# A fused attention and max-out kernel: one pair of loads ahead of the output weights, one product moved within a step, a table copied by GpSimd

## The chip, the cores and the metric

The kernel runs on one core of one Trainium2 chip. The time is the device time of one execution in microseconds (us). A core has five engines that run side by side, each with its instructions in a fixed order: TensorE (PE, with its weight loads shown apart as PEld), VectorE (DVE), ScalarE (ACT), GpSimd (POOL) and SyncE (SP). Data moves by DMA, issued here by SP (which also issues the DMA transposes) and by GpSimd (loads that turn float32 into bfloat16 on the way); ACT issues a few at the start.

## The reference

Two layers, the second fed by the first. There are 8 batches, 8 heads, 576 positions and 64 numbers a head:

```
scores = q @ k.T / 8 + bias[head, |i - j|]        # bias from a table of 32 buckets
x      = softmax(scores) @ v                      # (8 * 576) rows x 512
h      = max(x @ w1, x @ w2, x @ w3)              # 512 -> 768
out    = h @ w_out                                # 768 -> 512, float32
```

The bias depends only on the distance of two positions, and beyond a distance of 128 it is one constant. So exp(score + bias) is exp(score) times a factor that differs from one only in a band around the diagonal.

## The kernel before

**Tiles and steps.** Heads go in pairs. A step is one batch `b` and one pair `hp` (0 to 3). A batch's 576 positions are four tiles of 128 and 64 left over. In a step PE multiplies keys by queries in PSUM (`sc` for the main tiles, `sct` for the left-over keys, `scq` for the left-over queries), ACT writes the exponentials to SBUF (`e` for the main tiles, `el` for what is left over), VectorE multiplies the band by its factors (`times_band` and `times_band_pair`, lines 797 to 818, `times_bandt`, line 900, `times_band_left`, line 912), and PE multiplies by the values with a column of ones (`a`); VectorE then divides by that column's sum (`rd`, `x_sb`, lines 956 and 957). The product and the division of a step run during the next one (`attend`, line 920, called through `next_late`). `sc`, `sct` and `scq` take turns in two PSUM banks of the pool `ps_s`; ACT must have read a bank before PE writes it anew.

**Between these** stand the matmuls of the second layer for an earlier batch, in portions that `fill(target, *hooks)` (line 703) takes from a list: so many matmuls, with each hook (a product of the current step) called ahead of the last portion, or between two, and behind them if none is left. For the first batches the gates' tiles are `ps`, later `psp`; the products with the output weights are `pso`. The first of the latter come in the step of batch 2, pair 1, and read `wo_bf`.

**Band factors.** `hank` holds, for each head, the factors along the diagonals; it is read backwards. `bandt` holds the part for the left-over keys, copied once by `make_bandt` (line 346): two copies of 64 partitions by 768 numbers, each read backwards. In the kernel before, VectorE makes it in the first pass over batch 0's second halves (line 1152), before the first quotients. Its first reader is `times_bandt` of batch 0's first pair, line 901 in the profile.

**Loads.** From batch 2 on a batch's q and k come pair by pair: `load_pair(b, g)` issues two q and two k loads of 64 KB from GpSimd (line 189), `load_left` the left-over rows. `begin_qk(b)` issues pair 0, the left-over rows and pair 1, `end_qk(b)` pairs 2 and 3. Every load of a batch from 2 on goes through `in_turn` (line 150): once a list is open (`paced`, from batch 1 on), it waits for the sixth load before it to land. The weights' loads go through the same call with b = 0 and neither wait nor count. In the step of batch 1, pair 1, GpSimd issues the values of batch 2 (four main loads and two tails), then the output weights (`load_last_weights`, line 1079, 768 KB), then pairs 2 and 3 of batch 2. Two steps' code later come the loads for batch 3.

**Transposes.** From batch 2 on SP transposes q and k by DMA (line 725; left-over rows at line 732) at places written out by hand (`places`, line 1193): batch 2's pair 0 and left-over rows in the step of batch 1, pair 1, its pair 1 in that of pair 2, its third pair in that of batch 1, pair 3, its fourth pair in that of batch 2, pair 1. Between those two places stand the five transposes of batch 1's result, x to xT (line 967), two for the first half and three for the second. SP takes all of them in this order, and the stores of the output too. In this text "third pair" and "fourth pair" are the pairs of batch 2 with the numbers 2 and 3.

**The step of batch 2, pair 0** is the last one of its kind (no gates from a stage list, `rate` 8). There the left-over keys' product is not called in the first `fill`, as in other steps, but in the last one of the step, together with `times_bandt` (`late_keys`, `late_products`).

At the start, `load_second` (line 1066) issues batch 1's q and k in packed form (line 241), with left-over rows and the second weight matrix in between, has GpSimd spread the first pair (`spread_packed`, two copies, line 246), and issues batch 1's values and the third weight matrix.

Of the kernel before, what the change touches and what calls it, by code (L numbers as in the profile page):

```python
# [39 lines left out]
def kernel(  # L40
# [12 lines left out]
    nc = tc.nc  # L53
# [6 lines left out]
    HP = H // 2  # L60
# [63 lines left out]
    def dve_copy(out_, in_):  # L124
        return inorder(nc.vector.tensor_copy(out_, in_))
# [58 lines left out]
    def load_pair(b, g):  # L184

        for src, dst in zip((q, k), batch[b]):
            for par in range(2):
                part = main_part(src, b)[:, :, 2 * g + par, :]
                in_turn(b, nc.gpsimd.dma_start(out=dst[:, g, :, par, :], in_=part))  # L189
# [10 lines left out]
        load_left(b)  # L200
        load_pair(b, 1)

    def end_qk(b):
        for g in range(2, HP):
            load_pair(b, g)

    def go_behind(loads, behind):

        for load in loads if behind else ():
# [6 lines left out]
    def load_v(b, h0, h1):  # L216
        load_main(v, b, h0, h1, vx[b % 2][:, :, :, 0:D])
        load_tail(v, b, h0, h1, v_diag)
# [24 lines left out]
    def spread_packed(hp, eng):  # L243
        h = slice(2 * hp, 2 * hp + 2)
        for dst, src in zip(batch[1], (q_1, k_1)):
            inorder(eng.tensor_copy(dst[:, :, h, :], src[:, h].rearrange("p h t d -> p t h d")))
# [99 lines left out]
    def make_bandt():  # L346
        for par in range(2):
            r = slice(64 * par, 64 * par + 64)
            c = BAND // 2 - 64 * par
            dve_copy(bandt[r, :, :], hank[r, par::2, c : c + 192][:, :, ::-1])  # L350

# [546 lines left out]
    def times_bandt(hp, el):  # L900
        return inorder(nc.vector.tensor_tensor(
            out=el[:, S - 192 : S], in0=el[:, S - 192 : S], in1=bandt[:, hp, :], op=ALU.mult
        ))
# [153 lines left out]
    def load_w(i):  # L1057
        src = (moe_w1, moe_w2, moe_w3)[i].rearrange("(c p) f -> p c f", p=P)
        for f0, f1 in ((0, QS), (QS, d_ff)) if i else ((0, d_ff),):
            in_turn(0, nc.gpsimd.dma_start(out=w_bf[i][:, :, f0:f1], in_=src[:, :, f0:f1]))  # L1060
# [5 lines left out]
    def load_second():  # L1066
        for h0, h1 in ((0, 2), (2, H)):
            load_packed(k, h0, h1, k_1)
            load_packed(q, h0, h1, q_1)
            if h0 == 0:  # L1070
                load_q_tail(1)
                load_tail(k, 1, 0, H, k_diag)
                load_w(1)
        spread_packed(0, nc.gpsimd)
        load_v(1, 0, H)
        load_w(2)
# [16 lines left out]
    for hp in range(HP):  # L1093
        qT, kT = (x[:, hp, :] for x in qk[0])
        e4, el = e_tiles()
# [29 lines left out]
    for hp in range(HP):  # L1125
        qT, kT = (x[:, hp, :] for x in qk[0])
        if begun:
            e4, el = begun.pop()
            more_transposes(hp + 1)
            scores(qT, kT, e4, 1, 2)  # L1130
        else:
            e4, el = e_tiles()
            visit(qT, kT, e4, [(1, 0), (1, 2)], (lambda: more_transposes(hp + 1)) if hp + 1 < HP else None)

        def keys():
            left_keys(hp, qT, kT, el, QS, S)

        def queries():
            left_queries(hp, qT, kT, el)

        def late_bands(hp=hp, e4=e4):
            times_band(hp, e4, 1, QS, QM, inorder)
            times_band_pair(hp, e4, 2, QS)

        if hp == 0:
            keys()
        if hp == 1:
            x_transposes(0, 0)
        quotients = next_late()
        if hp < 2:  # L1150
            if hp == 0:
                make_bandt()
            quotients()
            if hp == 0:
                bands(2)
            else:
                behind.pop()()
                keys()
            queries()
            if hp == 1:  # L1160
                x_transposes(1, 0)
            else:
                begun.append(e_tiles())
                scores(*(x[:, 1, :] for x in qk[0]), begun[0][0], 1, 0)
            quotients = next_late()
            quotients()
            if hp == 0:
                bands(3)
            behind.append(lambda late_bands=late_bands, hp=hp, el=el: (late_bands(), products(hp, el)))
        else:  # L1170
            if behind:
                behind.pop()()
            if hp == 3:
                quotients()
                add_ffn(0, QS)
                fill(8)
            keys()
            if hp == 2:
                quotients()
            queries()  # L1180
            late_bands()
            if hp == 2:
                x_transposes(2, 0)
                x_transposes(3, 0)
            else:
                begin_qk(2)
                x_transposes(0, 1)
                fill(8, lambda: second_transposes(qk[1], 0))
            products(hp, el)
        late.append(lambda hp=hp, e4=e4, el=el: attend(0, hp, e4, el, 1))  # L1190
# [15 lines left out]
    for b, hp in [(b, hp) for b in range(1, B) for hp in range(HP)]:  # L1206
# [54 lines left out]
        if rows:  # L1261
            begin2, end2 = thirds.pop()()
            if not run.keys_late:
                end_keys = left_keys_rows(qT, kT, el)
            begin2()
            if not run.keys_late:
                end_keys()
            if not lead:
                key_scores(qT, kT, e4, 2)
            largest = end2(2 if run.keys_late else 1)  # L1270

            def bands():
                times_band(hp, e4, 2, 0, QM, inorder)
                times_bandt(hp, el)
                times_band(hp, e4, 3, 0, QM, inorder)

            def left():
                left_queries(hp, qT, kT, el)
                times_band_left(hp, el)

            def ahead():
                n = HP * b + hp + 1
                if n < HP * B:
                    begun.append(e_tiles())
                    key_scores(*(x[:, n % HP, :] for x in qk[n // HP]), begun[0][0], 0)

            run(
                lambda: key_scores(qT, kT, e4, 3), left, ahead, largest, bands, lambda: left_keys_rows(qT, kT, el)
            )
            thirds.append(after)  # L1290
        elif tiled:
            if len(pending) > 1:
                fill(DCH)
            keys()
            fill(FCH)
            times_band(hp, e4, 0, 0, QS, inorder)
            begin0, end0, begin1, end1, alone = run
            scores(qT, kT, e4, *order[2])
            begin0()
            exp_left = left_queries(hp, qT, kT, el)  # L1300
            turned_1 = begin1()
            if (b, hp) == (3, 0):
                left_keys(hp, qT, kT, el, 0, S)
            times_band(hp, e4, 1, 0, QM, inorder)
            band_left = times_bandt(hp, el)
            go_behind([band_left], turned_1[-1])
            times_band_left(hp, el)
            scores(qT, kT, e4, *order[3])
            dve0 = end0([exp_left])
            dve1 = end1([band_left])  # L1310
            times_band(hp, e4, 2, 0, QM, inorder)
            dve0()
            times_band(hp, e4, 3, 0, QM, inorder)
            dve1()
            pending.extend((n, [fn]) for n, fn in alone)
        else:
            late_keys = (b, hp) == (2, 0)
            fill(8 if (b, hp) == (2, 1) else rate, (lambda: None) if late_keys else keys, *([lambda: None] if together else []))
            if b == 1 and hp + 1 < HP:
                spread_packed(hp + 1, nc.vector)  # L1320
            if not late_keys:
                times_bandt(hp, el)


            def beside_scores():
                banks = [pool.tile([P, KT * 64], F32, tag=tag, name="scq") for pool, tag in ((ps_a, "a"), (ps_f, "ff"))]
                turn_left_queries(qT, kT, banks)
                put_left_queries(el, banks)

            visit(qT, kT, e4, order[2:], None if together else beside_scores, el=el if together else None)  # L1330
# [15 lines left out]
        if hp == 1 and b + 1 < B:  # L1346
            paced.append(b)
            load_v(b + 1, 0, H)
            if b == 1:
                load_last_weights()  # L1350
            end_qk(b + 1)
        if hp == (2 if b == 1 else 1) and b + 2 < B:
            begin_qk(b + 2)

# [5 lines left out]
                times_band(hp, e4, t, 0, QM, inorder)  # L1360

        if not tiled:
            def late_products():
                keys()
                times_bandt(hp, el)

            fill(rate, *([late_products] if late_keys else []), bands_2, queries)
            times_band_left(hp, el)
        if hp == 1 and b > 1:
            stages.extend(made)  # L1370
# [56 lines left out]
```

## Time and profile before

| What | Value |
|---|---|
| median of three runs (lowest, highest) | 309.41 us (309.14, 309.49) |
| the profiled execution: its own time | 309.08 us |
| the profiled execution: its span | 307.3 us |
| PE busy | 296.4 us (96%) |
| VectorE busy | 208.4 us (68%) |
| ACT busy | 201.9 us (66%) |
| GpSimd busy | 141.2 us (46%) |
| loads from GpSimd's queue | 16.66 MB |
| granted TensorE clock, mean | 0.997 |

The profile is of one execution. A busy share is an average over the span; where an engine stands still, and for what, is in other views. The *waits* name, for an engine and a line, what ended its idle time (total, number of times, longest). The *timeline* lists instructions in order of time: start, length, engine, line, what is written and read; a note in brackets is the idle time ahead of it and what ended that. For a DMA the length is that of its issue on the engine; its data lands later, and the trace has the time from issue to landing as well. The *chain* follows the work that ended last back from the end. Engines with a q behind the name (SPq) are their instruction queues. Line numbers are those of the kernel before.

### The profile page before, as it was taken

The numbers are of one execution on the slowest core, as the hardware profiler recorded it, in microseconds if no ns is written. First come the engines' busy times: TensorE is split into PE (matmuls) and PEld (weight loads), VectorE is DVE, ScalarE is ACT, GpSimd is POOL, SyncE is SP. The second block draws the span as 40 slices with busy tenths as digits, with TensorE's granted clock in tenths as the row PEclk, the third lists the DMA queues.
The fourth block names the chain that finished last, engine by engine and source line by source line (L and its number), as shares of the span: only waits on it lengthen the run. The fifth ranks groups of instructions, "written<-read, shape, count | busy, mean of one in ns | idle before, by whom it ended". The sixth has DMA issues, their size and how long they took to land.

```text
span 307.3 us, 10608 instructions
## 1 busy us (share of the span) xinstructions
PE 296.4 (96%) x4547; PEld 182.0 (59%) x4547; DVE 208.4 (68%) x471; ACT 201.9 (66%) x273; POOL 141.2 (46%) x197
## 2 busy tenths in 40 slices
PE   7889999999899999999999999999999999999995
PEld 2367877765455655567666766676667654444442
DVE  7498888776677767676777677767777765453552
ACT  3999989887677677768776777777777730222211
POOL 8977778479677657856566826510000000000000
PEclk9999999999999999999999999999999999999998
DMA  9999999999999999999999999996323013202003
GB/s 162 200 187 191 167 140 130 177 113 161 218 179 168 141 189 210 99 142 208 171 113 146 208 166 90 140 196 105 71 45 119 26 36 82 97 2 102 34 0 137
DMA packets 165774, 40.48 MB, mean 132 GB/s; under 512 B 154584, under 2 KB 161248, under 8 KB 165728
## 3 DMA queue, kind: packets, MB, share of 16 engines
q0 software_dynamic: 105664, 16.66, 91.0%
q1 hardware_dynamic: 58304, 22.69, 37.3%
q8 instruction: 35, 0.57, 0.8%
q10 hardware_dynamic: 1760, 0.47, 0.7%
q14 instruction: 11, 0.09, 0.1%
HBM read 35.39 MB, written 9.45 MB: 146 GB/s over the span
## 4 chain that ended last, share of the span: by engine, by line
PE 86%; ACT 6%; DMA 3%; SPq 2%; DVE 1%; issue 1%; ACTq 0%
PE psp L108 33%; PE ps L108 19%; PE a L108 13%; PE sc L108 9%; PE pso L108 5%; ACT e L821 4%; PE sct L108 2%; DMA kT<-k_sb 2%; PE warm L108 1%; PE scq L108 1%; SPq L967 1%; ACT el L821 1%; PE tp L112 1%; DMA out_dram<-osb 1%; PE xp L112 1%
## 5 line engine op out<-in xcount | busy, mean ns | idle before, releaser
L821 ACT ACTIVATE e<-sc 128x1024 bf16<-128x1024 f32 x128 | 128.6, 1026 | 31.5 <-PE sc L108 30.2
L108 PEld LDWEIGHTS <-w_bf 64*128 64x128 bf16 (+1 forms) x1088 | 73.8, 95 | 54.8 <-issue 1.1
L108 PE MATMUL psp<-xT,w_bf 64*128 64x512 bf16 x736 | 91.0, 376 | 0.0
L801 DVE TENSOR_TENSOR e<-e,hank 128x512 bf16<-128x512 bf16 (+2 forms) x120 | 56.1, 472 | 16.7 <-ACT e L821 16.0
L108 PE MATMUL ps<-xT,w_bf 128*128 128x512 bf16 (+1 forms) x352 | 65.1, 335 | 0.0
L108 PE MATMUL sc<-qT,kT 64*128 64x256 bf16 (+1 forms) x384 | 47.8, 306 | 3.8 <-DMA kT<-k_sb 1.5
L108 PEld LDWEIGHTS <-kT 64*128 64x128 bf16 (+1 forms) x736 | 30.6, 94 | 28.5 <-issue 9.1
L108 PE MATMUL a<-vx,e 64*128 64x65 bf16 (+1 forms) x1536 | 44.6, 191 | 0.0
L189 POOL DMA_DIRECT2D q_sb<-in_q_dram x48 | 36.1, 756 | 17.3 <-DMA vx<-in_v_dram 6.5
L189 POOL DMA_DIRECT2D k_sb<-in_k_dram x48 | 35.9, 755 | 16.8 <-DMA vx<-in_v_dram 11.0
L108 PEld LDWEIGHTS <-e 64*128 64x128 bf16 (+1 forms) x1536 | 40.7, 95 | 3.8
L108 PEld LDWEIGHTS <-hT 64*128 64x128 bf16 (+1 forms) x444 | 27.2, 95 | 19.2 <-DVE hT L545 1.3
L108 PE MATMUL a<-vt,el 64*128 64x65 bf16 (+1 forms) x240 | 30.8, 201 | 0.2 <-DVE m L505 0.2
L161 POOL DMA_DIRECT2D vx<-in_v_dram x28 | 24.7, 904 | 13.6 <-PE a L108 13.0
L415 ACT ACTIVATE m<-ps 128x512 bf16<-128x512 f32 x14 | 8.4, 597 | 34.3 <-PE ps L108 34.3
L821 ACT ACTIVATE el<-sct 128x576 bf16<-128x576 f32 (+2 forms) x36 | 21.7, 607 | 13.6 <-PE sct L108 12.4
L108 PEld LDWEIGHTS <-el 64*128 64x128 bf16 (+1 forms) x624 | 26.0, 95 | 7.8 <-issue 5.2
L108 PE MATMUL psp<-wo_bf,hT 64*128 64x256 bf16 (+1 forms) x336 | 29.7, 307 | 0.0
L108 PE MATMUL pso<-wo_bf,hT 128*128 128x512 bf16 (+2 forms) x108 | 23.2, 367 | 0.0
L424 DVE TENSOR_TENSOR m<-ps,m 128x512 bf16<-128x512 f32 x14 | 9.7, 692 | 17.0 <-PE ps L108 17.0
L821 ACT ACTIVATE el<-scq 128x512 bf16<-128x512 f32 (+1 forms) x38 | 19.5, 530 | 1.4 <-PE scq L108 1.3
L545 DVE TENSOR_TENSOR hT<-psp,m 128x1024 bf16<-128x1024 f32 (+1 forms) x16 | 14.9, 955 | 6.6 <-PE psp L108 6.6
(82 smaller groups left out, 295.0 us busy)
## 6 DMA issues: line engine op xcount, KB each, us to landing
out_dram<-osb SPq DMA_DIRECT2D x35, 256.0 KB, 4.2
vx<-in_v_dram POOLq DMA_DIRECT2D x28, 128.0 KB, 6.1
q_sb<-in_q_dram POOLq DMA_DIRECT2D x50, 64.0 KB, 5.3
k_sb<-in_k_dram POOLq DMA_DIRECT2D x48, 64.0 KB, 4.7
w_bf<-in_moe_w_dram POOLq DMA_DIRECT2D x2, 512.0 KB, 8.3
xT<-in_k_dram SPq DMA_DIRECT2D x6, 128.0 KB, 4.6
hank<-w_dr SPq DMA_DIRECT2D x2, 384.0 KB, 5.6
w_bf<-in_moe_w_dram POOLq DMA_DIRECT2D x1, 768.0 KB, 9.4
```

The source lines that it names most:

```text
L108: made = inorder(nc.tensor.matmul(*args, **kw))
L112: inorder(nc.tensor.transpose(*args))
L161: in_turn(b, nc.gpsimd.dma_start(out=dst[:, t, h0:h1, :], in_=x[:, t, h0:h1, :])) for t in range(t0, t1)
L189: in_turn(b, nc.gpsimd.dma_start(out=dst[:, g, :, par, :], in_=part))
L415: nc.scalar.activation(out=st[fb]["m0"][:], in_=ps0, func=ACTF.Copy)
L424: inorder(nc.vector.tensor_tensor(out=m[:], in0=ps1, in1=st[fb]["m0"][:], op=ALU.max))
L545: inorder(nc.vector.tensor_tensor(out=out_[:, i : i + n], in0=ps2()[:, i : i + n], in1=m[0][:, i : i + n], op=ALU.max,))
L801: put(nc.vector.tensor_tensor(out=e4[:, t, :, lo:hi], in0=e4[:, t, :, lo:hi], in1=hank[:, 2 * hp : 2 * hp + 2, c0:c1][:, :, ::-1], op=ALU. ...
L821: made = nc.scalar.activation(out=out_, in_=in_, func=ACTF.Exp, scale=inv_sqrt_d)
L967: inorder(nc.sync.dma_start_transpose(out=xT[:, :, c : c + w], in_=x_sb[b][P - w :, t, :]))
```

## The change

Three edits. First, the loads of batch 2's third pair go ahead of the output weights' load, and those of the fourth pair stay behind it; for other batches the order is what it was. Second, the left-over keys' product of batch 2, pair 0, and its band factors go back to where other steps have them: the first `fill` and right behind it. Third, `make_bandt` copies on GpSimd, and is called in `load_second` behind the second weight matrix.

```diff
-    def end_qk(b):
-        for g in range(2, HP):
-            load_pair(b, g)
...
-            dve_copy(bandt[r, :, :], hank[r, par::2, c : c + 192][:, :, ::-1])
+            inorder(nc.gpsimd.tensor_copy(bandt[r, :, :], hank[r, par::2, c : c + 192][:, :, ::-1]))
...
                 load_w(1)
+                make_bandt()
...
-            if hp == 0:
-                make_bandt()
             quotients()
...
-            late_keys = (b, hp) == (2, 0)
-            fill(8 if (b, hp) == (2, 1) else rate, (lambda: None) if late_keys else keys, *([lambda: None] if together else []))
+            fill(8 if (b, hp) == (2, 1) else rate, keys, *([lambda: None] if together else []))
             if b == 1 and hp + 1 < HP:
                 spread_packed(hp + 1, nc.vector)
-            if not late_keys:
-                times_bandt(hp, el)
+            times_bandt(hp, el)
...
             load_v(b + 1, 0, H)
+            load_pair(b + 1, 2)
             if b == 1:
                 load_last_weights()
-            end_qk(b + 1)
+            load_pair(b + 1, 3)
...
-            def late_products():
-                keys()
-                times_bandt(hp, el)
-
-            fill(rate, *([late_products] if late_keys else []), bands_2, queries)
+            fill(rate, bands_2, queries)
```

In the order of instructions that results, GpSimd has the two copies between the fifth weight issue and the load that follows it; VectorE's first `times_bandt` waits for GpSimd. PE has two matmuls of `sct` (512 and 64 columns) between two blocks of eight `ps` matmuls, where they stood behind the second block and the scores; ACT has their exponential ahead of the step's third one over the main tiles. GpSimd's load of the weights stands four loads later.

## The prediction

> **What bounds the kernel now.** I read the page first: PE is busy for 96% of the span, and the chain that ended last is 86% PE, so what counts is where PE stands still or is held up. Then the longest waits in the window from 56 to 82 us, which are few:
>
> ```profile
> PEld L108 <- DMA kT<-k_sb: 2.0, 1, 2.0
> PE sc L108 <- DMA kT<-k_sb: 1.5, 1, 1.5
> ```
>
> One transfer, the transposed keys of one pair of heads, stops PE once (columns: total, times, longest). The timeline of PE has it at 79.31 to 80.81, ahead of the scores of batch 2's last pair (1.49 us). The timeline of SP shows where that transfer was late (start, length, instruction):
>
> ```profile
> 50.31 1.73 SPq L725 DMA_TRANSPOSE kT<-k_sb  x1
> 62.94 1.90 SPq L725 DMA_TRANSPOSE qT<-q_sb  x1
> 64.94 1.21 SPq L725 DMA_TRANSPOSE kT<-k_sb  x1
> 66.31 6.48 SPq L967 DMA_TRANSPOSE xT<-x_sb  x5
> 72.91 1.20 SPq L725 DMA_TRANSPOSE qT<-q_sb  x1
> 74.22 2.05 SPq L725 DMA_TRANSPOSE kT<-k_sb  x1
> ```
>
> SP issues in order. It has nothing to issue from 52.04 to 62.94 (SP's own waits: 43.0 us in two waits on q loads, the longest 32.1, so 10.9 for this one); then the third pair, five transposes of batch 1's results and the fourth pair follow one another without a gap. Of these 13 us only the start waited for data: the third pair's q. Why q was late stands in the timeline of GpSimd:
>
> ```profile
> 50.56 0.92 POOL L1079 DMA_DIRECT2D wo_bf<-in_moe_w_out_dram  x1
> 52.30 0.76 POOL L189 DMA_DIRECT2D q_sb<-in_q_dram  x1 [0.81 <-DMA vx<-in_v_dram]
> 53.92 0.74 POOL L189 DMA_DIRECT2D q_sb<-in_q_dram  x1 [0.86 <-DMA vx<-in_v_dram]
> 55.11 0.74 POOL L189 DMA_DIRECT2D k_sb<-in_k_dram  x1 [0.45 <-DMA vx<-in_v_dram]
> 56.82 0.74 POOL L189 DMA_DIRECT2D k_sb<-in_k_dram  x1 [0.97 <-DMA vx<-in_v_dram]
> 57.55 1.50 POOL L189 DMA_DIRECT2D q_sb<-in_q_dram  x2
> 62.75 1.49 POOL L189 DMA_DIRECT2D k_sb<-in_k_dram  x2 [3.70 <-DMA q_sb<-in_q_dram]
> ```
>
> By their landing times, one by one: the output weights 11.7 us after issue (62.3), the q behind them 10.2 (62.5), the two k 8.2 and 7.0 (63.3, 63.8). Everything behind the weights lands right after them; the same 64 KB at 43 us landed in 3.4 to 3.8.
>
> **The loads (part 1).** No instruction is added. The third pair's four loads wait for the four v loads, not for the weights, so they issue at the same 52.30 to 56.82; the weights' issue moves from 50.56 to about 57.55, and the fourth pair's loads follow at 58.5. The two v tails ahead of them land by 57.3 (50.0 + 7.3). Then q and the first k come at about 58, the second k at the earliest 56.82 + 3.8 = 60.6. SP issues the third pair at about 58.5 and 60.6 in place of 62.94 and 64.94. Behind it stand the five xT transposes, whose inputs VectorE writes at 60.23 to 60.65 and 63.13 to 63.69: they take 61.8 to 68.3. The fourth pair's k waited 3.70 us for the third pair's q and loses that wait; its transposes go out at 68.4 and 69.7 in place of 72.91 and 74.22. With the same 6.5 us to land, kT is there at 76.2, three us before PE asks at 79.31. The stall of 1.49 goes whole. Next after it is PE itself: the following pair at 88.94 starts without a gap after the same kind of matmuls. SP's later transposes (batch 3, from 78.02) move ahead too. **-1.5 us** (ends 0 and -1.5).
>
> What it puts at risk is the weights. They are first read at
>
> ```profile
> 66.70 1.46 PE L108 MATMUL pso<-wo_bf,hT 128*128 128x512 bf16 x6
> ```
>
> 4.4 us after they land today. Issued at 57.55, they land at 66.95 if like the first weight matrix, of the same 768 KB (9.4 us at 15.21); at 69.25 if as slow as now; at 60.6 + 5.3 = 65.9 if they take the queue for as long as now (57.0 to 62.3) once the last k is in. Against the early ends speaks that SP's transposes then run beside them, which they don't from 52 to 62.9 now; against the late end that 11.7 counts 6.4 us behind v and its tails. I take 66 to 67; PE asks at 66.70 - 0.4 + 1.1 = 67.4 (parts 2 and 3): **0** (ends 0 and +1.85, which is 69.25 - 67.4).
>
> **The left-over keys (part 2).** In batch 2's first pair their product `sct` (0.41 on PE, 0.65 on ACT) moves from 62.51 to about 60.1, between two blocks of eight `ps` matmuls; its inputs landed at 54.5 (47.62 + 6.9). The score banks are two and used in turn. Today the next pair's scores stand behind both banks: PE idles 63.79 to 63.92 for an exponential, and the second four matmuls start at 64.46, after the left-over keys' own exponential ends at 64.36. In the new order that exponential lies in ACT's idle 0.60 ahead of 61.38, the next bank is free at 62.4 and the second when the pair's last exponential ends, at about 63.95: 64.46 - 63.98 = 0.48. VectorE's products follow the same exponentials and have 0.46 and 0.76 idle here, so no one else is late. **-0.4** (ends 0 and -0.5).
>
> **The band factors (part 3).** VectorE loses two copies (0.71 us at 17.46). That gains nothing: the next instruction there, at 18.35, waits 0.18 for PE, which waits for ACT's exponentials. GpSimd gets them behind the fifth weight issue and ahead of the load at 24.92:
>
> ```profile
> 21.64 0.75 POOL L1060 DMA_DIRECT2D w_bf<-in_moe_w_dram  x1 [0.52 <-DMA vx<-in_v_dram]
> 24.92 0.82 POOL L241 DMA_DIRECT2D xT<-in_k_dram  x1 [2.53 <-DMA w_bf<-in_moe_w_dram]
> 26.70 0.62 POOL L246 COPY q_sb<-xT 128x512 bf16<-128x512 bf16 x1
> ```
>
> So they start at 22.39, in 2.53 us of idle time that also shields the loads behind them. But they have a reader at once (VectorE):
>
> ```profile
> 22.14 0.68 DVE L816 TENSOR_TENSOR e<-e,hank 128x1024 bf16<-128x1024 bf16 x1
> 22.74 0.25 DVE L901 TENSOR_TENSOR el<-el,bandt 128x192 bf16<-128x192 bf16 x1
> 26.43 1.55 DVE L901 TENSOR_TENSOR el<-el,bandt 128x192 bf16<-128x192 bf16 x1
> ```
>
> L901 gets a wait that wasn't there, with all of VectorE behind it: L914, the quotients, the next pair's bands. VectorE has no idle time from 18.35 to 29.6 in which to catch up. The price of a copy isn't in the trace: the nearest row on GpSimd is 0.62 for 512 elements a partition, so 0.93 for 768; VectorE's own 0.35 is the low end. Two are 1.86: the factors are there at 24.25, or at 24.68 if the copies first stand behind L816 (ends 22.82). The third line shows that the two engines hold each other up: L901 takes 1.55 in place of 0.25 beside GpSimd's two copies at 26.70 to 27.87.
>
> PE's path: the second half of the first attention product starts at 23.34; its second nine matmuls read what L901 wrote, at about 24.8 in place of 23.64. The product then ends about 1.15 late (25.4, not 24.25). PE's wait of 0.29 at 24.84 swallows part: 0.86. The next such product (26.14) needs its own L901 and L914, which now come at 26.6 and meet GpSimd's copies at 26.70: 0 to 0.7 more. From 25 us the chain is PE's own, so this stays. **+1.1**. Low end 0 (copies at 0.35: factors at 23.1, in time for 23.64); high end 1.6, all of the meeting.
>
> [...]
>
> **Sum.** -1.5 - 0.4 + 1.1 + 0 = **-0.8 us**. The profiled execution took 309.08 us (span 307.3); the median of the three runs shown is 309.41, within 0.1% of it, so I take the change from the profile to the median: 308.6 us.
>
> **Rivals.** *A, the weights come too late.* The 1.49 us is given back at 66.70: with 11.7 us from issue, PE waits there until 69.25, 2.55 later than today; the gains and losses before that place vanish in this wait, the stall at 79.31 goes: +1.1, 310.5 us. The time is level when the weights land at 68.2, and beyond 68.8 it is slower. For it: SP's transposes run beside them now. Against it: 9.4 for the same size. *B, the copies cost nothing:* -1.5 - 0.4 = -1.9, 307.5 us; for it VectorE's 0.35 for such a copy, against it the 0.62 of GpSimd for a smaller one. *C, the copies eat the gain:* 1.3 us each (half as slow again as the row, or the meeting at 26.70 in full), +1.9 on PE: 309.4 us, up to 309.9.
>
> **Chances.** Forecast (-1.3 to -0.3) 0.52; A (0 to +2) 0.20; B (-2.2 to -1.3) 0.15; C (0 to +0.5) 0.13. A measurement of this kernel can tell about 0.2%, 0.62 us, from no change. Faster by more: 0.36 of the forecast's and all of B, 0.51. Slower by more: 0.15 of A and 0.02 of C, 0.17. Within: 0.32. Range: 307.7 leaves out half of B, 310.3 some 0.12 of A. The forecast's own range is 308.1 to 309.1.
>
> **What would show it.** Right: no wait of PE on kT near 79; the third pair's transposes before 61; the weights landed before the first `pso`; `sct` at 60; L901 near 24.6 with GpSimd as its releaser, and PE about one us late at 28. Wrong: PE waiting for `wo_bf`; the copies far from 0.9 us each; the L901 of the second pair stretched to 1.5 us.

## The result, and the profile after

The changed kernel took 310.58 us (median of 17 runs, 308.86 to 311.95); the kernel before, on the same chip and in turn with it, 309.49 us (17 runs, 307.94 to 313.37). The ratio is 1.0045 with a 95% interval of 1.0024 to 1.0067: slower by about 1.4 us by the ratio (the medians lie 1.1 apart), where 0.8 us less was forecast. The profiled execution took 309.92 us (span 308.2; before 309.08 and 307.3). Most lines of code behind line 205 or so have numbers smaller by 4 now (L725 is L721, L901 is L897), some by 3 (L1079 is L1076).

Up to 80 us the changed kernel gains what it was meant to gain. In the timeline of SP the third pair's transposes come ahead of 61 us; the fourth pair's still stand behind the five xT, and its kT goes out at 72.70, 1.5 us earlier than before:

```profile
57.99 1.24 SPq L721 DMA_TRANSPOSE qT<-q_sb  x1
59.95 1.26 SPq L721 DMA_TRANSPOSE kT<-k_sb  x1
61.38 9.05 SPq L963 DMA_TRANSPOSE xT<-x_sb  x5
70.54 1.20 SPq L721 DMA_TRANSPOSE qT<-q_sb  x1
72.70 1.19 SPq L721 DMA_TRANSPOSE kT<-k_sb  x1
```

PE's wait of 1.49 us for keys near 79 us is gone (first the kernel before, then the changed one). The keys landed at 78.56, 0.7 us before PE asked for them:

```profile
80.81 0.61 PE L108 MATMUL sc<-qT,kT 64*128 64x256 bf16 x8 [1.49 <-DMA kT<-k_sb]
```

```profile
79.26 0.60 PE L108 MATMUL sc<-qT,kT 64*128 64x256 bf16 x8
```

I set the two profiles side by side by the order of PE's weight loads, which is nearly the same in both, and read how much later the changed kernel starts the same one: 0.13 us earlier at 20 us, 0.57 later from 30 to 60 us (the copies), 0.11 later at 70 us (the left-over keys), 1.55 earlier from 84 to 150 us. So at 150 us the change had gained more than the forecast gave it. From 160 us to the end it is 0.9 us later. These 2.45 us are lost in two places (the idle times in brackets, 0.80 and 1.31, count from modelled ends of matmuls and are shorter than what the starts lose), which the timeline of PE shows (first the changed kernel, then the same place in the kernel before):

```profile
149.50 1.25 PE L108 MATMUL psp<-xT,w_bf 64*128 64x512 bf16 x10
151.55 0.82 PE L108 MATMUL psp<-xT,w_bf 64*128 64x512 bf16 x6 [0.80 <-issue]
...
155.97 0.30 PE L108 MATMUL sct<-qT,kT 64*128 64x288 bf16 x2
157.57 0.39 PE L108 MATMUL sc<-qT,kT 64*128 64x512 bf16 x2 [1.31 <-ACT el L817]
```

```profile
151.06 1.90 PE L108 MATMUL psp<-xT,w_bf 64*128 64x512 bf16 x16
...
156.68 0.39 PE L108 MATMUL sc<-qT,kT 64*128 64x512 bf16 x2
```

The sixteen products of a gate break into ten and six with 0.80 us between them. "issue" says that nothing in the profile released the six: the ten ahead of them read the same two tiles. The 1.31 us is put down to ACT by the profile, but the kernel before has the same matmuls without any wait, and the section on what stops PE shows that it is the same kind of stop.

Two more views belong to this. The queue of loads on GpSimd has fallen behind (columns: start, length of the issue; in brackets the idle time ahead of it and what ended it):

```profile
57.34 0.83 POOL L1076 DMA_DIRECT2D wo_bf<-in_moe_w_out_dram  x1
58.15 1.52 POOL L189 DMA_DIRECT2D q_sb<-in_q_dram  x2
59.63 1.52 POOL L189 DMA_DIRECT2D k_sb<-in_k_dram  x2
61.10 1.54 POOL L189 DMA_DIRECT2D q_sb<-in_q_dram  x2
68.25 0.74 POOL L189 DMA_DIRECT2D k_sb<-in_k_dram  x1 [5.62 <-DMA q_sb<-in_q_dram]
70.70 0.74 POOL L189 DMA_DIRECT2D k_sb<-in_k_dram  x1 [1.70 <-DMA q_sb<-in_q_dram]
...
80.01 3.53 POOL L161 DMA_DIRECT2D vx<-in_v_dram  x4
```

The loads of batch 3's first pair start behind the fourth pair's, and its first k waits 5.62 us for a q that stands behind the output weights; its left-over rows and its second pair follow, and the values of batch 3 at 80.01, where the kernel before has

```profile
65.67 1.53 POOL L189 DMA_DIRECT2D k_sb<-in_k_dram  x2
...
73.24 3.54 POOL L161 DMA_DIRECT2D vx<-in_v_dram  x4
```

The delay shrinks but lasts: the values of batch 4 are issued at 104.0 (98.8 before), of batch 5 at 132.0 (126.1), of batch 6 at 158.7 (156.0, after 3.67 us of waiting for PE).

The DMA engines have a lull near each of the two stops, but that alone does not tell the kernels apart. The DMA view has a queue "instruction", 35 packets of 16 KB in the whole run. One of them runs from 149.00 to 150.17, and one from 155.07 to 156.17. Around the first the view of half a microsecond reads, for 149.0 to 149.5 and for 150.0 to 150.5 of the changed kernel:

```profile
q8 instruction: 1, 0.02, 14.6%
```

```profile
DMA packets 14, 0.00 MB, mean 6 GB/s; under 512 B 14, under 2 KB 14, under 8 KB 14
```

The kernel before has the same lull around its own packet of 147.48 to 148.90, and PE does not stop there; from 149.0 to 149.5, and from 150.0 to 150.5 when it is over, it reads

```profile
DMA packets 18, 0.00 MB, mean 9 GB/s; under 512 B 18, under 2 KB 18, under 8 KB 18
```

```profile
DMA packets 604, 0.10 MB, mean 194 GB/s; under 512 B 604, under 2 KB 604, under 8 KB 604
```

### The profile page after: what moved, and what is told of

It reads as the page before. It is cut to its first block, busy times and chain, and to the rows that moved or that the text cites. A ratio compares the mean times of both kernels' runs of the same rounds, so it can differ in the third digit from the quotient of the medians.

```text
span 308.2 us, 10611 instructions
## 1 busy us (share of the span) xinstructions
PE 296.2 (96%) x4547; PEld 181.7 (59%) x4547; DVE 207.1 (67%) x469; ACT 202.0 (66%) x273; POOL 143.3 (47%) x199
## 4 chain that ended last, share of the span: by engine, by line
PE 83%; POOL 5%; ACT 4%; DMA 3%; DVE 2%; issue 2%; POOLq 0%; DVEq 0%; ACTq 0%
PE psp L108 34%; PE ps L108 18%; PE a L108 13%; PE sc L108 8%; PE pso L108 6%; PE sct L108 2%; DMA vx<-in_v_dram 2%; ACT e L817 2%; ACT el L817 1%; POOL q_sb L161 1%; PE scq L108 1%; POOL ktail L180 1%; POOL bandt L346 1%; DMA out_dram<-osb 1%; POOL vx L296 0%
## 6 DMA issues: line engine op xcount, KB each, us to landing
vx<-in_v_dram POOLq DMA_DIRECT2D x28, 128.0 KB, 6.7
xT<-in_k_dram SPq DMA_DIRECT2D x6, 128.0 KB, 4.4
```

## Experiments: which of the three edits it is

The theory after the result, T1: the new order of loads makes the stream of loads late; late loads fall into the stretch where PE works off its code fastest, and PE waits for its code there. The rivals: the copies on GpSimd cost it all (T2), or the stops are chance that any kernel has (T3). The numbers in brackets behind a ratio are its 95% interval; a ratio is not exactly the quotient of the medians beside it. The comparison is always the kernel before, measured anew with each group of runs, so its median differs from group to group. The first four runs take the edits apart. Loads alone:

```diff
             load_v(b + 1, 0, H)
+            load_pair(b + 1, 2)
             if b == 1:
                 load_last_weights()
-            end_qk(b + 1)
+            load_pair(b + 1, 3)
```

> The kernel before with one part of the change: the third pair's q and k loads ahead of the output weights, the fourth pair's behind them. T1 (the load stream): the fourth pair's loads come later, the loads of batch 3 on are issued some 6 us later (v of batch 3 at 80 instead of 73 us), and what the early stages gain (1.5 us at 80 us) is lost again between 140 and 165 us, where the code fetches and the loads meet: 309.8 to 310.7 against 309.5, ratio 1.001 to 1.004. T2 (the copies on GpSimd cost it all): the 1.5 us are kept, 308.0, ratio 0.995. T3 (the stalls near 150 us hit any kernel in some executions): some 308.5, ratio 0.997, and stalls of PE without a wait for an engine's result in the profiles of kernels with the old order too.

Measured: 310.67 against 309.24 us, ratio 1.0047 (1.0020 to 1.0073). The load order alone costs all that the change costs; T2 is out. Its profile repeats the two stops, the first shorter and the second longer:

```profile
151.62 0.82 PE L108 MATMUL psp<-xT,w_bf 64*128 64x512 bf16 x6 [0.49 <-issue]
158.74 0.39 PE L108 MATMUL sc<-qT,kT 64*128 64x512 bf16 x2 [2.40 <-issue]
```

Here the second, at the same matmuls that the profile put down to ACT in the changed kernel, is put down to nothing. Keys alone:

```diff
-            late_keys = (b, hp) == (2, 0)
+            late_keys = False
```

> The kernel before with only the left-over keys of batch 2 in their usual place. All theories: the second scores of the step at 64 us no longer wait for their keys, -0.4 us there; but PE meets the wait for the keys near 79 us behind it, which then takes the 0.4 back: 309.1 to 309.5, ratio 0.9985 to 1.000. The start of the second half's code fetches and loads is that of the kernel before.

Measured: 308.54 against 309.24 us, ratio 0.9986 (0.9959 to 1.0014). In its profile PE gains 0.47 us between 60 and 68 us, as in the changed kernel. The wait for keys near 79 us was still 1.38 us, so it did not take the 0.47 back, as I had expected it to: keys and PE both came earlier. Copies alone:

```diff
-            dve_copy(bandt[r, :, :], hank[r, par::2, c : c + 192][:, :, ::-1])
+            inorder(nc.gpsimd.tensor_copy(bandt[r, :, :], hank[r, par::2, c : c + 192][:, :, ::-1]))
```

with the call in `load_second` as in the change.

> The kernel before with only the band factors' copies on GpSimd. T1: PE is 0.6 us later at 27 us as in the changed kernel, but the wait for the keys at 79 to 81 us is still there and takes it up in part: 309.5 to 310.1, ratio 1.000 to 1.002. T2: the copies cost all that the change lost and gained, 310.6 to 312, ratio 1.004 to 1.008. T3: 309.5 to 310.1 as in T1.

Measured: 309.12 against 309.24 us, ratio 1.0013 (0.9978 to 1.0048). PE is 0.8 us later behind the copies, and no longer behind 84 us, since the wait for keys did not come. That was not because PE was late: the keys landed at 78.85, ahead even of the 79.31 at which the kernel before asks for them. Loads and keys without the copies (the two diffs above together):

> The changed kernel with the band factors' copies back on VectorE: loads and keys alone. T1 (the load stream): as the loads alone or 0.3 below, 309.4 to 310.5, ratio 1.000 to 1.003. T2 (the copies): 307.6 to 308.0, ratio 0.994 to 0.995. T3 (chance): 308.1 to 308.6, ratio 0.996 to 0.997.

Measured: 310.05 against 309.24 us, ratio 1.0031 (1.0002 to 1.0060), with one stop of 1.58 us at 156.8. Loads, keys and copies add up: +0.47%, -0.14% and +0.13% make 0.46%, and the change measured 0.45%. That they meet so closely is luck: each of the three is known to about 0.3%, and keys and copies are not told from nothing.

## Experiments: what stops PE

A stop that nothing releases could be PE waiting for its own instructions (its code). If PE starves for its code, the stops must depend on where a piece of code ends. The next two kernels cut the 17 warming matmuls of the first 15 us, 512 columns each, into four of 128; that puts 102 more instructions ahead of the rest, and no cost of it shows (308.27 against 308.70 us with nothing else changed, below).

```diff
-            mm(out_, lhsT=zeros[:, 0:P], rhs=zeros[:])
+            for c in range(0, CH, P):
+                mm(out_[:, c : c + P], lhsT=zeros[:, 0:P], rhs=zeros[:, c : c + P])
```

With loads and keys of the change:

> Loads and keys of the change, band factors on VectorE, and the 17 warming matmuls of 512 columns in the first 15 us each cut into four of 128: the same columns, 102 more PE records ahead of all the rest, so each 16 KB piece of PE's code starts some 100 records earlier in the program (a piece is about 253 records by the profiles so far). The loads go as in the run with loads and keys alone. T1a (the stalls near 150 and 157 us come where a code fetch that waits behind loads meets the records that PE eats fastest): the two stalls change, each by more than 0.5 us or away, and the time moves with them, 307.5 to 309.5, ratio 0.994 to 1.000. T1b (the late load stream costs PE's time itself, whatever the code): still 2 us lost between 140 and 165 us, 309.5 to 310.5, ratio 1.001 to 1.004.

With nothing else changed:

> The kernel before with the same cut of the warming matmuls: nothing of the loads is changed. T1a: its code pieces meet the loads elsewhere, so stalls of PE without an engine's result to wait for may turn up where the kernel before has none: 308.5 to 311, ratio 0.998 to 1.006, whatever comes is told by such stalls alone. T1b: no change, ratio 0.999 to 1.001, 309.2 to 309.6.

Measured: 310.77 against 308.70 us, ratio 1.0050 (1.0014 to 1.0085), for the first; 308.27 us, ratio 0.9973 (0.9936 to 1.0011), for the second. The first profile has small stops only (0.20 us at 146.4, 0.33 at 202.3) and took 308.48 us, which is 2.3 below the kernel's own median: one execution without much loss, while the other executions lose more. The medians do not decide between T1a and T1b of these two expectations; the first median is above the range of both. What decides is where PE stops. In the 18 profiles of this case I counted PE's records (matmuls, weight loads, and the 50 waits and drains that its queue shows) up to each stop of 0.12 us or more between 85 and 260 us. Leaving out one that sits between the same matmuls in all profiles (0.17 us, at 121 to 125), and two in one kernel that waited for transposes (i_later, below; their counts do not fit the others), 28 are left. Their counts are 4289, 4545, 4801, 5825, 6081, 6849 and 7105, which differ by multiples of 256 without exception (in the profiles where 13 records are missing, 8 less). The extra 102 instructions changed nothing in that: the stops stayed at the same counts, which are other matmuls of the program. And each time PE went on 1.3 to 1.7 us after a 16 KB packet of the instruction queue had ended. So a packet holds 256 of PE's instructions (35 packets for 9144 records in the kernel before), and PE stops at the end of one piece until the next is there. That what stops PE is its code is thus shown.

How late the packet comes differs between the profiles. From PE's last record before the boundary at 4545 to the start of the next packet it took 1.69 us in the kernel before, 4.69 in the changed kernel, 5.48 with loads alone; PE needs 4.65 us for the piece in between when nothing stops it (151.93 to 156.58 in the kernel before). In the 15 profiles whose warming matmuls are whole, the stop at 4801 goes with this delay: none of 0.12 us or more at 1.69 to 2.28 us, 0.24 at 2.51, 0.40 at 2.86, 1.35 to 1.58 at 3.94 to 4.07, 2.13 at 4.72; where PE had already stopped at 4545 it is smaller for its delay (1.31 at 4.69 in the changed kernel). Why the packet starts late is the question of the next section.

## Experiments: is it the lateness of the loads?

The kernel before in its own order, with the first load of batch 3 held back until the load just ahead of it has landed:

```diff
-                go_behind([load], in_flight[-DEEP])
+                first = b == 3 and not third
+                go_behind([load], in_flight[-1 if first else -DEEP])
+            if b == 3:
+                third.append(load)
```

> The kernel before in its own order, only that the first load of batch 3 waits for the last load issued before it instead of for the one six before: the load stream from there on is late by some 5 us, as in the changed kernel. T1 (a late stream is enough): code fetches near 145 to 158 us take 5 us or more from PE's reaching of a piece to the packet's start, against 2.4 and 4.1 in the kernel before, and PE stalls there by 1 to 2.5 us: 310.4 to 312, ratio 1.003 to 1.008. The rival (the order of the pairs itself, and not the lateness): no stall there, 309.0 to 309.7, ratio 0.999 to 1.001.

Measured: 309.55 against 308.70 us, ratio 1.0008 (0.9978 to 1.0038). The delay came out smaller than meant: v of batch 3 at 76.75, of batch 6 at 157.0. The stop is there, with the order of pairs as it was:

```profile
156.61 0.39 PE L108 MATMUL sc<-qT,kT 64*128 64x512 bf16 x2 [1.35 <-ACT el L824]
```

The median stayed in the rival's range, though, and a repeat of the kernel before (m1_before, below) has such a stop without any hold, so this run decides little. The same with three such holds (`alone = b == 3 and len(third) in (0, 4, 7)`):

> The kernel before in its own order; three of batch 3's loads (the first of its first pair, the first of its left-over queries and keys, the first of its second pair) each wait for the load issued just before. The stream falls behind in three steps instead of one; the run with one such wait had v of batch 3 at 76.8 us, v of batch 6 at 157.0 (156.0 in the kernel before) and one stall of 1.35 us. T1 (the later the stream, the more PE waits for its code near 150 to 160 us): v of batch 6 at 159 us or later, PE stalls of 2 us or more, always behind the same records (16 or 17 pieces in), 310.5 to 312.5, ratio 1.004 to 1.010. The rival (a matter of the order of the pairs or of chance): 308.7 to 309.7, ratio 0.999 to 1.002.

Measured: 313.33 against 309.97 us, ratio 1.0118 (1.0074 to 1.0162). That is more than expected, since the stream now was so late (v of batch 3 at 86.5) that PE also waited 1.32 us for a transpose at 110.0 and 1.70 at 115.7. So its median does not weigh the stop alone. The stop at the end of the piece came on top of it:

```profile
161.27 0.39 PE L108 MATMUL sc<-qT,kT 64*128 64x512 bf16 x2 [2.13 <-issue]
```

The reverse, loads and keys of the change with a deeper window for batch 3:

```diff
-            if len(in_flight) >= DEEP and paced:
-                go_behind([load], in_flight[-DEEP])
+            deep = DEEP + 4 if b == 3 else DEEP
+            if len(in_flight) >= deep and paced:
+                go_behind([load], in_flight[-deep])
```

> Loads and keys of the change, band factors on VectorE, and batch 3's loads wait for the load ten before them instead of six, so that the stream need not wait 6 us behind the output weights near 62 us. T1: v of batch 3 is issued at 74 to 76 us instead of 80, the code fetches near 145 to 158 us wait no longer than in the kernel before, and the early gain is kept: 307.4 to 308.2, ratio 0.993 to 0.997. The rival (the transfers and not the window set the stream): v at 79 to 80 us, the stalls as in the run of loads and keys, ratio 1.001 to 1.004.

Measured: 311.11 against 308.70 us, ratio 1.0051 (1.0016 to 1.0085), a stop of 1.85 us at 158.6; PE also waited 1.47 us for transposed results (xT) at 76.73. The rival was right on the window: v of batch 3 is issued at 77.2 to 80.0, because the transfers themselves are late, so T1 was not put to the test. In the profiles 2.79 MB move from 50 to 72 us after the change and 3.21 MB before; in the kernel before SP issues no transpose from 52.0 to 62.9, and GpSimd's queue moves 1.48 MB (of 1.79 in all) in that time; in the changed kernel it moves 1.07 (of 1.37) in the same 10.9 us. Why the new order moves less there isn't settled; no run took the transposes away from the weights' side.

The kernel before without the load of the output weights at all (the last products read other weights, so its output is not the reference's), which gives the third pair its early loads and delays nothing:

```diff
-                load_last_weights()
...
-rhs=wo_bf[:, cf, c0:c1],
+rhs=w_bf[0][:, cf % DCH, c0:c1],
```

> The kernel before without the load of the output weights (0.77 MB); the last products read the first product's weights in their place, so the output is not the reference's, while every instruction but that one load is as before. The third pair's loads thus come as early as the change put them, and nothing comes later for it. T1: no wait for keys near 80 us (1.5 us less, as in the changed kernel), v of batch 3 at 70 us or before, v of batch 6 at 153 to 156 us (waiting for PE), no stall of PE near 150 to 158 us: 307.2 to 308.0 in the median, ratio 0.992 to 0.996. The rival (an earlier PE meets these stalls whatever the loads do): stalls of 1.5 us or more there, 309 to 310, ratio 0.999 to 1.003.

Measured: 307.96 against 309.97 us, ratio 0.9953 (0.9931 to 0.9975), within what T1 expected; v of batch 3 at 71.3, of batch 6 at 155.2, one stop of 0.24 us, and no wait for keys:

```profile
80.06 0.60 PE L108 MATMUL sc<-qT,kT 64*128 64x256 bf16 x8
```

So the early keys are worth having where they do not push the loads back; how much of the gain is the 768 KB less to move is not shown. And with loads and keys of the change, a shallower window in the very stretch of the stops:

```diff
+            if b == 6:
+                sixth.append(load)
+            deep = 4 if b == 6 and len(sixth) < 12 else DEEP
...
-                go_behind([load], in_flight[-DEEP])
+                go_behind([load], in_flight[-deep])
```

> Loads and keys of the change, band factors on VectorE, and the first eleven loads of batch 6 (issued near 140 to 156 us) wait for the load four before instead of six. T1b (a code fetch waits for the loads that are in flight at its time): the fetches there start 4 us or less after PE reaches its piece instead of 6, the stalls shrink to below 0.8 us in sum, 308.0 to 309.2, ratio 0.996 to 1.000, though the stream is later still (v of batch 6 at 160 us or later). T1c (the number in flight does not matter, only how busy the DMA engines are, or what else is in their queues): stalls as in the run with loads and keys, 309.5 to 311, ratio 1.001 to 1.006.

Measured: 310.96 against 309.97 us, ratio 1.0028 (1.0001 to 1.0056). T1b and T1c of this expectation both got half. For T1b, the two stops shrank to 0.28 and 0.21 us, with v of batch 6 at 161.8, and the packet behind the boundary at 4545 started 3.16 us after it, against 4.07 with loads and keys alone. For T1c, the median: PE lost the same later, with stops of 0.22, 0.70 and 0.69 us at the counts 5825, 6081 and 7105: the late loads met other pieces instead. Whether a packet waits for the loads in flight or for the DMA engines in general stays open. One version that might have been better than both, left-over keys in their usual place and cut warming matmuls in the old load order:

> The left-over keys in their usual place, the loads in the old order, and the warming matmuls cut in four: the two edits whose ratios were below 1 so far (0.9986 and 0.9973, neither certain). T1: the load stream is as early as in the kernel before and the pieces of code end elsewhere: 307.8 to 308.6, ratio 0.994 to 0.998. If both were chance: ratio 0.999 to 1.001.

Measured: 309.30 against 309.97 us, ratio 0.9985 (0.9960 to 1.0010). No version here was faster beyond doubt but the one without the weights.

## Experiments: how sure was the wait of 1.49 us?

Three profiles with the old load order (f_before_phase, g_late, i_later) had no wait for keys near 79 us at all. So each of the two kernels ran twice more.

> The kernel before once more, one execution with a profile. If the 1.5 us wait for keys near 79 us, which the forecast counted as a sure gain, stands in every execution, it is here too (1.0 to 1.6 us). If it is there only when a code fetch falls on the fourth pair's transposes (near 74 us in the first profile), it is here in about half of the cases: of six other profiles with the old order and PE in time, two had it and three had not, and one could not tell. Stalls for code between 140 and 165 us: none or below 0.6 us.

> The same a second time, with the same two answers: a wait of 1.0 to 1.6 us near 79 us in both, or in one or none; stalls for code between 140 and 165 us of none or below 0.6 us.

Measured: 309.73 and 308.47 us; no wait of PE for keys in either. In the two profiles with a wait of 1.4 us or more a packet of PE's code lay on the issue of the fourth pair's kT (73.95 to 75.18 on 74.22 in the first); j_keys_phase waited 0.95 without that, so what brings the wait is not settled. The scores that waited until 80.81 in the profile that the forecast used stand at 79.37 in the first, with PE in time. But that execution has the other stop, which I had not expected in the kernel before at this size:

```profile
79.37 0.61 PE L108 MATMUL sc<-qT,kT 64*128 64x256 bf16 x8
...
157.03 0.39 PE L108 MATMUL sc<-qT,kT 64*128 64x512 bf16 x2 [1.58 <-ACT el L821]
```

> The changed kernel once more. If the stalls for code come with its late load stream: v of batch 6 issued at 157 us or later, 1.3 to 3.3 us lost by PE between 148 and 160 us, PE standing still behind the same records as before (piece 16 or 17). If they were chance: none, and 307.5 us.

> The same a second time: stalls of 1.3 to 3.3 us between 148 and 160 us and v of batch 6 at 157 us or later, or, by chance, none and 307.5 us.

Measured: 309.52 us with one stop of 1.85 us at 157.2 (count 4801), and 312.48 us with two:

```profile
153.14 0.82 PE L108 MATMUL psp<-xT,w_bf 64*128 64x512 bf16 x6 [1.64 <-issue]
159.71 0.39 PE L108 MATMUL sc<-qT,kT 64*128 64x512 bf16 x2 [1.85 <-issue]
```

The values of batch 6 came at 158.3 and 160.5. Every profile of the changed kernel has the stops.

All profiles together, by how late the loads are against PE: the time at which GpSimd could issue v of batch 6 (its start less its wait for PE), plus what PE is ahead of the first profile at 140 us; and what PE lost from 140 to 170 us, both against the first profile.

| Kernel | Lateness, us | PE lost, us |
|---|---|---|
| b_keys | 149.8 | 0.0 |
| j_keys_phase | 151.2 | 0.3 |
| f_before_phase | 151.3 | 0.8 |
| e_phase | 151.5 | 0.4 |
| before | 152.3 | 0 |
| c_band | 152.4 | 0.6 |
| m2_before | 155.1 | 0.1 |
| k_no_wo | 155.7 | 0.4 |
| m1_before | 157.0 | 1.8 |
| g_late | 157.5 | 1.5 |
| n1_after | 160.0 | 2.2 |
| d_loads_keys | 160.1 | 1.8 |
| after | 160.2 | 2.5 |
| h_deep | 161.2 | 2.2 |
| n2_after | 161.3 | 3.9 |
| l_shallow (window cut) | 162.9 | 0.8 |
| a_loads | 163.0 | 3.3 |
| i_later | 163.2 | 2.5 |

Below 156 the loss is at most 0.8 us, above it at least 1.5, but for the kernel whose window was cut just there. Lateness counts against PE: in m1_before v of batch 6 could be issued 3.2 us later than in the kernel's first profile (155.5 for 152.3), PE is 1.4 us earlier because it did not wait at 79 us, and it pays 1.8. The lateness is not an effect of the stops: taken in the same way at the values of batch 5, some 20 us ahead of them, it parts the kernels alike, 128.0 or less without a large loss and 128.1 or more with one, again but for l_shallow. The border is thin there (m2_before 128.0, m1_before 128.1). T3 is right in so far as the stops can come in the kernel before; the new order makes them the rule.

The sum closes, as far as 13 executions can tell. In the seven profiles with the old order and an untouched stream (before, m1_before, m2_before, b_keys, c_band, f_before_phase, j_keys_phase) the wait for keys was 1.49, 1.38 and 0.95 us in three and none in four, 0.55 on average; from 140 us to the end PE lost 0.67 on average. In the six with the new order and an untouched stream (after, n1_after, n2_after, a_loads, d_loads_keys, e_phase) the wait was never there, and PE lost 2.49, from 1.05 (e_phase) to 4.2 (n2_after). That is -0.55 + 1.8 = +1.3 us for the loads; loads alone measured +1.4.

## Why the prediction was wrong, step by step

- **The loads, -1.5: here it failed, twice.** The third pair's transposes and the end of the wait came as written: SP at 57.99 and 59.95 for 58.5 and 60.6, no wait near 79. The fourth pair's did not: qT and kT went out at 70.54 and 72.70 for 68.4 and 69.7, and kT landed at 78.56 for 76.2. The five xT took 9.05 us in place of 6.5, and the pair's second k landed only at 72.65, 12.3 us after its issue. The step had given these loads a start behind the weights but no late landing; that the wait went all the same was by 0.7 us, not three. The size was that of one execution. The wait stood in three of seven profiles, so the term was worth about 0.55 us. And the step looked at what is late next only on PE and on SP ("next after it is PE itself"; "SP's later transposes move ahead too"). Nothing was put in for the loads behind the fourth pair, whose issue waits for landings. The weights landed 4.3 us later (66.5 for 62.2) and what stood behind them later still: the first k of batch 3 was issued 2.6 us later (65.67 to 68.25), v of batch 3 6.8 us later, and PE paid 1.8 us for it on average, seventy microseconds on. The queue was followed on SP and not on GpSimd.
- **The weights, 0: right.** Landed 9.2 us after issue, at 66.54, and the first `pso` started at 66.81 without a wait (forecast: 66 to 67, and 67.4), with 0.3 us to spare. One of the other profiles with the new order (l_shallow) waited 0.70 us there, so rival A was near, but it was not what made the kernel slower.
- **The left-over keys, -0.4: right.** `sct` at 60.54, and 0.46 us gained between 60 and 68 us, 0.47 alone.
- **The band factors, +1.1: right in mechanism, and on average somewhat too high.** The changed kernel's profile shows the copies and VectorE's new wait:

```profile
21.96 2.15 POOL L346 COPY bandt<-hank 64x768 bf16<-64x768 bf16 x2
```

```profile
22.13 1.30 DVE L812 TENSOR_TENSOR e<-e,hank 128x1024 bf16<-128x1024 bf16 x1
24.15 0.26 DVE L897 TENSOR_TENSOR el<-el,bandt 128x192 bf16<-128x192 bf16 x1 [0.72 <-POOL bandt L346]
```

  The copies took 1.08 us each (0.88 in n1_after) for the 0.93 of the row. L812 began 0.17 us behind the first and took 1.30 in place of 0.68: it was the copies' neighbour in place of L901. In n2_after the two began together; there L812 took its 0.68, that copy 1.35 and the other, later, 0.82. So the two do hold each other up. Which of them goes on first is not shown: in the kernel before L901 started first, at 26.43 against 26.70, took its 1.55 us and ended behind the two copies (27.98 against 27.87). From 20 to 30 us PE lost 0.70, 0.38 and 1.53 us in three executions of the changed kernel, and 0.76 with the copies alone.
- **Rivals and chances.** The rival that ended slower had another mechanism than the one that came. That a later part of the kernel could take a gain back was not among the cases; the range ended at 310.3, and slower beyond doubt had been given 0.17.

## What to carry to other kernels

A load that is moved ahead of a large one can make every load behind both late (here v of batch 3 by 6.8 us): follow the queue on until it has caught up, not to the next reader. Where one profile shows a wait of a transfer that comes 1 us late, look at a second execution before the wait is counted as a gain. Where DMA has no free time (here its engines are busy for 90% or more of each slice of the profile up to some 207 us), a gain of PE can be taken back far behind the edit, and PE's own code is one of the transfers that come late (4.69 us behind the boundary at 4545, for 1.69 before).

## What the runs showed of the hardware

PE's code comes by DMA in packets of 16 KB, 35 in a run, and PE's stops for it lie multiples of 256 records apart. The packets start 3.45 to 12.56 us apart until 250 us in the kernel before, 3.82 to 10.97 in the changed one. Where PE has stopped for one, it goes on 1.3 to 1.7 us after the packet has ended (1.38 and 1.40 in the changed kernel). Around the end of many of them the other transfers almost stop (6 GB/s from 150.0 to 150.5 in the changed kernel, 177 GB/s from 151.0 to 151.5), but not around all: in the kernel before 302 GB/s moved from 142.0 to 142.5, behind its packet of 141.21 to 142.09. What makes the difference is not shown. The piece behind 4545, in which 90 of the products are short (64 partitions, 65 columns), takes PE 4.65 us in the kernel before; a packet that started 1.69 us after that boundary left it running, one that started 2.51 us after it cost 0.24 us, one at 5.48 us cost 2.4. The profile's labels for such a stop are "issue" or the engine that happened to finish last (ACT in four of the profiles).

Most crossings from one piece to the next cost nothing that the profiles show: between 85 and 260 us, 422 of 450 have no stop of 0.12 us or more. The other 28 cost 0.12 to 2.4 us each, in 16 of 18 profiles, and such crossings are what this change lost by.
